# Rows in parity order, so that the first and last DFT steps and the transposes of h run on half-array tiles

## The chip, the cores and the metric

One NeuronCore of a Trainium2 chip. The metric is the device time of one execution in microseconds (us), median over runs. Engines: PE is TensorE, PEld its weight loads, DVE the vector engine, ACT ScalarE, POOL GpSimd; SyncE (SP) issues the DMA transfers. An execution's "span" is the profiled one and is 1 to 2 us shorter than the time. The granted clock is the share of TensorE's full clock that the profile records.

## The reference

2048 rows of 640 numbers in bf16. Two branches share the rows x = q, and a gate mixes them row by row:

```python
k_shift = sum over 4 taps of shifted k * shift_k           # short causal convolution
kv = k_shift * v
y  = irfft(rfft(kv, 2S) * rfft(ssm_k, 2S))[:S] + kv * ssm_D  # long convolution
a  = q * y
h  = gelu(layernorm(x) @ w1); hs = shifted quarters of h @ w2
x1 = x + hs;  b = x1 + gelu(layernorm(x1) @ w3) @ w4
out = g * a + (1 - g) * b,   g = sigmoid(x @ gate_w)
```

The kernel does the transforms as matmuls with tables in four steps: F1 (step 1), T2, I, F4 (step 4). Between steps 1 and 2 and between 3 and 4 the data go out to scratch in DRAM (S_x, S_h, S_g) and are gathered from there in another order. q is loaded a second time for the end; these are the "q reloads".

## The kernel before

Partition p holds the 16 consecutive rows 16p to 16p + 15, so a load takes DRAM in 128 pieces. Step 1 treats even and odd p apart: the table `F1[:, r, :]` has zeros in the rows of the other parity, so each of its matmuls spends all 128 rows and half of them are zeros. Step 4 likewise weaves two results together with a table half of whose columns are zeros. A hand-made list, `ORDER`, fixes the order of all steps.

```python
q_rows = A_q.rearrange("b (p t1) d -> (b p) t1 d", t1=NT)          # k_rows, v_rows, o_rows alike
SP.dma_start(out=X[:, 4*c:4*c+4, :], in_=q_rows[:, 4*c:4*c+4, :])   # 128 rows outermost
...
# h_transpose, per half of 16 steps
for i in range(8):
    PE.transpose(out=ps[:, i, :], in_=hv[:, 8*hh + i, :], identity=IDB[:])
...
# step 1, tasks u < 4 (the fifth has two matmuls of 256 columns)
PE.matmul(ps, lhsT=F1[:, u % 2, :], rhs=src[:, o + 512*(u//2):o + 512*(u//2) + 512], ...)
...
# step 4
for r in range(2):
    PE.matmul(ps[:], lhsT=F4[:, r] (two halves woven, one of them zero), rhs=g[:, r, ... 320], start=(r == 0), stop=(r == 1))
...
def store(t1): SP.dma_start(out=o_rows[:, t1, :], in_=X1[:, t1, :])
def load_q(c): SP.dma_start(out=q2[:], in_=q_rows[:, 4*c:4*c+4, :])   # q again, for the end
```

## Time and profile before

| | before |
|---|---|
| time, median (range) | 250.67 us (250.34 to 251.15) |
| span | 249.1 us |
| V chunk wanted by the vector engine | 32.6 us |
| first product of spectra starts | 123.0 us |
| last product ends | 208.5 us |
| first matmul of step 4 | 223.5 us |
| last vector or ScalarE instruction ends | 246.3 us |

The last five rows are instants read in the trace. They cut the span into stages: front, products, third transforms, tail. With the cuts as windows (columns: stretch, length, busy us of PE, PEld, DVE, ACT, POOL, clock, DMA share, GB/s):

```profile
0.00:20.00 20.00, 7.62 (x104) 6.75 (x105) 16.55 (x53) 14.33 (x22) 1.66 (x11) 1.00 0.91 350
20.00:123.00 103.00, 100.92 (x771) 56.69 (x771) 86.28 (x236) 92.68 (x153) 9.61 (x16) 0.98 0.85 247
...
208.50:223.50 15.00, 15.00 (x101) 8.10 (x99) 5.04 (x8) 3.65 (x4) 0.00 (x0) 1.00 0.38 129
```

TensorE is full from 20 to 123 us and from 208.5 to 223.5; before 20 us the loads are what is full (DMA share 0.91, 350 GB/s).

### The profile page before, as it was taken

How to read it: one execution, taken by the hardware profiler on the slowest of the kernel's cores; microseconds unless marked ns; L12 is line 12 of the kernel's file. 1: busy time of each engine (PE TensorE's matmuls, PEld its weight loads, DVE VectorE, ACT ScalarE, POOL GpSimd, SP SyncE). 2: the span in 40 equal slices, each digit the busy share in tenths (PEclk: the TensorE clock that was granted, in tenths of full speed). 3: DMA queues.
4: the chain of work that ended last, by engine and by line, in shares of the span. 5: the costliest groups of instructions: out<-in, count | busy, mean ns of one | idle time of the engine just before them, and what ended most of it. 6: DMA issues, size and time to landing. Idle time of an engine off the chain costs nothing. (4 is left out here: it accounts for less than half of the span.)

```text
span 249.1 us, 4377 instructions
## 1 busy us (share of the span) xinstructions
PE 227.3 (91%) x1637; PEld 128.6 (52%) x1637; DVE 212.2 (85%) x425; ACT 177.9 (71%) x292; POOL 11.3 (5%) x26
## 2 busy tenths in 40 slices
PE   0746999999999999999999899999989989999994
PEld 0735564444477555444555355555544546546652
DVE  6989998549995999985899999999999997508995
ACT  5599996984699999999988958845678460144530
POOL 1003301000000100031000000000000000000000
PEclk9997999999999999999999999999999999999999
DMA  6999897968858959995997618998403953268773
GB/s 250 377 416 291 189 216 167 240 256 263 241 217 243 387 204 233 346 381 146 183 304 215 204 64 251 186 366 302 132 3 101 342 218 105 105 237 281 222 265 108
DMA packets 50980, 57.65 MB, mean 231 GB/s; under 512 B 25610, under 2 KB 42763, under 8 KB 50703
## 3 DMA queue, kind: packets, MB, share of 16 engines
q1 hardware_dynamic: 50958, 57.38, 74.5%
q8 instruction: 13, 0.21, 0.4%
q14 instruction: 9, 0.07, 0.1%
HBM read 33.77 MB, written 18.36 MB: 209 GB/s over the span
## 5 line engine op out<-in xcount | busy, mean ns | idle before, releaser
L782 PE MATMUL ps<-W,gt 128*128 128x512 bf16 (+1 forms) x384 | 56.6, 299 | 0.0
L764 PE MATMUL ps<-x1t,W 128*128 128x512 bf16 x240 | 55.1, 379 | 0.0
L782 PEld LDWEIGHTS <-gt 128*128 128x128 bf16 x384 | 30.3, 98 | 23.2 <-issue 1.1
L769 ACT ACTIVATE gt<-ps 128x1024 bf16<-128x1024 f32 x24 | 24.5, 1041 | 20.3 <-PE ps L764 20.2
L764 PEld LDWEIGHTS <-W 128*128 128x128 bf16 x240 | 23.3, 98 | 26.4 <-issue 0.3
L323 DVE CAST stg<-ps 128x512 bf16<-128x512 f32 x41 | 26.4, 683 | 5.5 <-PE ps L370 5.3
L639 PE MATMUL psm<-xt,WA 128*128 128x512 bf16 x100 | 23.4, 379 | 0.0
L407 PE MATMUL ps<-ax,TB 128*128 128x512 bf16 (+3 forms) x128 | 22.5, 299 | 0.6 <-DVE hs L323 0.4
L321 ACT CAST stg<-ps 128x512 bf16<-128x512 f32 x39 | 21.7, 602 | 1.2 <-PE ps L370 1.1
L716 PE MATMUL psw<-WA,HT 128*128 128x512 bf16 (+1 forms) x116 | 21.6, 299 | 0.0
L321 ACT CAST gs<-ps 128x512 bf16<-128x512 f32 x29 | 15.2, 599 | 7.5 <-PE ps L446 7.5
L321 ACT CAST xs<-ps 128x512 bf16<-128x512 f32 x27 | 14.7, 617 | 7.0 <-PE ps L407 5.0
L321 ACT CAST hs<-ps 128x512 bf16<-128x512 f32 x27 | 14.2, 601 | 3.2 <-PE ps L407 3.2
L407 PEld LDWEIGHTS <-TB 128*128 128x128 bf16 x128 | 11.6, 98 | 9.2 <-issue 1.9
L784 DVE SCALAR_TENSOR_TENSOR X<-ps,OMG,X 128x640 bf16<-128x640 f32 x16 | 14.0, 877 | 2.4 <-PE ps L782 2.4
L718 DVE SCALAR_TENSOR_TENSOR X<-psw,X 128x640 bf16<-128x640 f32 x16 | 13.1, 819 | 3.3 <-PE psw L716 3.3
L522 PE MATMUL psk<-DG,KT 64*128 64x256 bf16 (+3 forms) x190 | 11.1, 250 | 5.0 <-ACT yk L530 3.7
L815 DVE SCALAR_TENSOR_TENSOR q<-ps,GS,q 128x320 bf16<-128x320 f32 x15 | 7.8, 542 | 9.0 <-PE ps L805 9.0
L639 PEld LDWEIGHTS <-WA 128*128 128x128 bf16 x100 | 9.5, 98 | 11.5 <-issue 0.7
L809 ACT ACTIVATE y<-ps,GS 128x320 bf16<-128x320 f32 x17 | 8.1, 525 | 9.7 <-PE ps L805 7.3
L716 PEld LDWEIGHTS <-HT 128*128 128x128 bf16 x116 | 10.1, 98 | 9.5 <-issue 0.7
L642 ACT ACTIVATE HT<-psm 128x1024 bf16<-128x1024 f32 (+1 forms) x12 | 10.5, 888 | 6.1 <-PE psm L639 5.9
(147 smaller groups left out, 386.3 us busy)
## 6 DMA issues: line engine op xcount, KB each, us to landing
S_x<-stg SPq DMA_DIRECT2D x8, 640.0 KB, 4.3
ax<-S_x SPq DMA_DIRECT2D x8, 640.0 KB, 5.3
S_h<-stg SPq DMA_DIRECT2D x8, 640.0 KB, 9.0
ax<-S_h SPq DMA_DIRECT2D x8, 640.0 KB, 5.3
S_g<-gs SPq DMA_DIRECT2D x8, 640.0 KB, 5.7
W<-in_B_w_dram SPq DMA_DIRECT2D x2, 1920.0 KB
KV<-in_A_v_dram SPq DMA_DIRECT2D x4, 640.0 KB, 11.6
gin<-S_g SPq DMA_DIRECT2D x4, 640.0 KB, 6.5
```

The source lines that it names most:

```text
L321: A.copy(out=dst, in_=src)
L323: V.tensor_copy(out=dst, in_=src)
L407: PE.matmul(ps[:, a - 512 * u:b - 512 * u], lhsT=st["T2"][:, 4 * s + i, :], rhs=ax[:, i, a - i * D:b - i * D], start=True, stop=True)
L522: PE.matmul(ps[e][:, lo:hi, :], lhsT=kt[a], rhs=st["DG"][a, 4 * k + lo - i:4 * k + hi - i, a], start=(i == 0), stop=(i == 7))
L639: PE.matmul(ps[:, v, :].rearrange("p (a b) -> p a b", a=4), lhsT=W1N[:, k, 160 * f:160 * f + P] if f < 4 else W1M[:, k, :], rhs=xt[:, :, k ...
L642: A.activation(out=st["HT"][:, 4 * c:4 * c + 4, 2 * u:2 * u + nf, :].rearrange("p t f b -> p f t b"), in_=ps[:].rearrange("p f (t b) -> p ...
L716: PE.matmul(ps[:, o:o + w], lhsT=h_tile(f, t1), rhs=W2P[:, f, o:o + w], start=(f == 0), stop=(f == 4))
L718: V.scalar_tensor_tensor(out=X1[:, t1, :], in0=ps[:], scalar=1.0, in1=X[:, t1, :], op0=ALU.mult, op1=ALU.add, accum_out=S12[:, 0, t1:t1 + 1])
L764: PE.matmul(ps[:, u, :].rearrange("p (a b) -> p a b", a=4), lhsT=st["W3"][:, k, f * P:(f + 1) * P], rhs=xt[:, :, k, :], start=(k == 0), st ...
L769: A.activation(out=gt[:, 2 * (fp % 2):2 * (fp % 2) + 2, :], in_=ps[:], func=ACT.Gelu_apprx_tanh)
L782: PE.matmul(ps[:, o:o + w], lhsT=st["gt", c, f // 4][:, f % 4, i * P:(i + 1) * P], rhs=st["W4"][:, f, o:o + w], start=(f == 0), stop=(f == ...
L784: V.scalar_tensor_tensor(out=X1[:, t1, :], in0=ps[:], scalar=OMG[:, t1:t1 + 1], in1=X1[:, t1, :], op0=ALU.mult, op1=ALU.add)
```

## The change

The intent is to stop multiplying by zeros. If the even p (blocks of 16 rows) lie in partitions 0 to 63 and the odd ones in 64 to 127, then step 1 is two matmuls of 64 rows on the upper and lower half of the array, side by side, and step 4 two matmuls of 64 columns. For that, every load and store must put the rows in parity order, and the transposes of h must come out so.

```diff
-    q_rows = A_q.rearrange("b (p t1) d -> (b p) t1 d", t1=NT)      # and o_rows, v_rows, k_rows
+    def rows(T, t, n):
+        return bass.AP(tensor=T.tensor, offset=T.offset + t * D, ap=[[NT * D, 2], [2 * NT * D, H], [1, n * D]])
-        SP.dma_start(out=X[:, 4 * c:4 * c + 4, :], in_=q_rows[:, 4 * c:4 * c + 4, :])
+        SP.dma_start(out=X[:, 4 * c:4 * c + 4, :], in_=rows(A_q, 4 * c, 4))     # likewise K, V, q again, out
 h_transpose:
-                    PE.transpose(out=ps[:, i, :], in_=hv[:, 8 * hh + i, :], identity=IDB[:])
+                    for r in range(2):
+                        PE.transpose(out=ps[H * r:H * r + H, i, :], in_=hv[:, 8 * hh + i, r, :], identity=IDB[:], tile_position=(0, H * r))
 step1:
-                    PE.matmul(ps..., lhsT=F1[:, u % 2, :], rhs=src[:, o + 512 * (u // 2):...], ...)
+                for r in range(2):
+                    PE.matmul(ps[r][:], lhsT=F1[H * r:H * r + H, :], rhs=src[H * r:H * r + H, o + 512 * u:o + 512 * u + 512], ...)
 step4:
-                    PE.matmul(ps[:], lhsT=F4[:, r].rearrange("p a b -> p (a b)"), rhs=g[:, r, ...], start=(r == 0), stop=(r == 1))
+                    PE.matmul(ps[H * r:H * r + H, :], lhsT=F4[:], rhs=g[:, r, ...], start=True, stop=True, tile_position=(0, H * r))
# cut: tables F1 and F4 without the zeros, h_shift's copies in parity order, K chunk 0 loaded and transposed
# on TensorE instead of by a transposing DMA, and a new ORDER of all steps
```

H is 64, NT 16, D 640.

## The prediction

The gaps marked in it are passages that no trace or run of this case shows: rules for how many DMA engines a pattern gets and how much tiles gain, and a clause that gave the engines numbers. No term is cut with them: the sum came to 431 us of span, and each of its terms stands in the text. "Two of 16 engines" is the author's estimate, from one load of the kernel before: the W2 tail, with a slowest dimension of 4, had 5 completion events and was in 1.9 us after the load issued before it; by its packets of 55 ns 4 engines would need 1.8 us and 16 engines 0.4.

> **What bounds the kernel now.** I read the page's engine totals and the 40 slices first, then a table by stretches, then the groups by form, the chain, and last the DMA side.
>
> ```profile
> PE 227.3 (91%) x1637; PEld 128.6 (52%) x1637; DVE 212.2 (85%) x425; ACT 177.9 (71%) x292; POOL 11.3 (5%) x26
> PE   0746999999999999999999899999989989999994
> ...
> DMA  6999897968858959995997618998403953268773
> GB/s 250 377 416 291 189 216 167 240 256 263 241 217 243 387 204 233 346 381 146 183 304 215 204 64 251 186 366 302 132 3 101 342 218 105 105 237 281 222 265 108
> ```
>
> TensorE is busy in nine tenths of every slice from 25 us on. Before that the DMA row is full and TensorE is not: the loads set the first 20 us. The stretches say where the vector engine (DVE) is nearly as full:
>
> ```profile
> 10.00:20.00 10.00, 5.53 (x87) 4.65 (x85) 8.78 (x22) 9.97 (x15) 0.45 (x1) 1.00 1.02 412
> ...
> 120.00:200.00 80.00, 77.28 (x491) 41.54 (x489) 77.94 (x78) 57.45 (x97) 0.00 (x0) 1.00 0.72 204
> ...
> 224.00:249.00 25.00, 21.42 (x158) 13.26 (x156) 21.00 (x52) 8.76 (x18) 0.00 (x0) 1.00 0.65 219
> ```
>
> Columns: stretch, length, busy us of PE, PEld, DVE, ACT, POOL, clock, DMA share, GB/s. From 120 to 200 us (the products) DVE has 77.9 of 80 us, as much as PE. In the last 25 us both have 21. The DMA share 1.02 at 412 GB/s says that all 16 DMA engines run without a gap from 10 to 20 us: 412/16 = 25.75 GB/s for each.
>
> ```profile
> DVE 23%; PE 18%; issue 2%; ACT 0%; ACTq 0%; DVEq 0%
> ```
>
> The chain names DVE ahead of PE and covers under half of the span, so I weigh stages, not this list. Its lesson is only that PE time saved will not all come off.
>
> **The work that the change touches on PE:**
>
> ```profile
> L370 PE MATMUL ps<-HT,F 128*128 128x512 bf16 x32 | 10.1, 379 | 0.3 <-ACT stg L321 0.3
> L370 PE MATMUL ps<-KV,F 128*128 128x512 bf16 x32 | 10.0, 379 | 0.6 <-DVE stg L323 0.4
> L805 PE MATMUL ps<-gin,F 128*128 128x320 bf16 x64 | 9.8, 299 | 0.0
> L522 PE MATMUL psk<-DG,KT 64*128 64x256 bf16 x100 | 9.6, 276 | 5.0 <-ACT yk L530 3.7 <-ACT KT L321 1.3
> ```
>
> The means there overlap, so I took start-to-start distances in the trace: 216 ns for 512 columns, 136 for 320, 109 for 256, 63 for a transpose of h. The last row already uses two row tiles (64*128), and there the two partners start 3 ns apart; the column-tiled rows of z start 2 to 4 ns apart. So pairs do run side by side in this kernel.
>
> **The DMA side:**
>
> ```profile
> KV<-in_A_v_dram SPq DMA_DIRECT2D x4, 640.0 KB, 11.6
> ...
> out_dram<-X SPq DMA_DIRECT2D x16, 160.0 KB, 3.1
> ...
> X<-in_A_q_dram SPq DMA_DIRECT2D x3, 640.0 KB, 9.2
> ...
> WA<-in_B_w_dram SPq DMA_DIRECT2D x1, 640.0 KB, 5.6
> ...
> WA<-in_B_w_dram SPq DMA_DIRECT2D x1, 160.0 KB
> ```
>
> Each 640 KB load is 128 packets of 5120 B, 8 on each of 16 engines. A packet of 5120 B takes 196 ns in the trace, of 2560 B 103, of 1280 B 55. The last line shown is the key witness. It loads the tail of W2 through a pattern whose slowest DRAM dimension is 4, not 128:
>
> ```profile
> 44.46 0.58 SPq L171 DMA_DIRECT2D WA<-in_B_w_dram  x1
> 45.08 0.74 SPq L172 DMA_DIRECT2D WA<-in_B_w_dram  x1
> ```
>
> By the trace's landing records the first (640 KB, 128 rows outermost) has 16 completion events and is in at 50.07 us. The second, a quarter as large, has 5 events, the first at once (1.13 us after issue), and is in at 51.96 us, 1.9 us later. On 4 engines its 128 packets of 1280 B are 32 each, 32 x 55 ns = 1.8 us; on 16 they would be 0.4 us.
>
> [...] 16 events for 128 rows, 4 + 1 for the dimension of 4, 1 + 1 for the one-row transfers of z. [...]
>
> **The change part by part.**
>
> 1. Step 1: before 64 matmuls of 512 columns and 32 of 256: 64 x 0.216 + 32 x 0.109 = 17.3 us. After, 40 pairs of row tiles of 512: 40 x 0.216 = 8.6. Saved 8.7 us of PE. Evacuations stay 80 of 512 columns or the like.
> 2. Step 4: 64 x 0.136 = 8.7 us become 32 pairs, 4.35. Saved 4.35, but in the last 25 us, where DVE has 21 us of its own: I count 2.
> 3. Transposes of h: 80 x 63 ns = 5.0 us become 160 of half the size in column pairs: no change if the pairs overlap.
> 4. K's chunk 0 goes through PE: 20 transposes of 56 to 107 ns, +1.1 to 2.1 us, with DVE copies. The new order gives ACT some 8 us more and DVE 4 us less (207 to 208): small.
> 5. Loads and stores. To get the rows in parity order, all loads of X, K, V and q and all stores use a DRAM pattern [2][64][n x 640], on chip 128 partitions. [...] the same bytes on two of 16 engines, 64 packets each. A 640 KB load takes 64 x 196 ns = 12.5 us instead of 1.6; a store 64 x 55 ns = 3.5 us instead of 0.44.
>
> **Front.** Down to the last V load, those two engines get 11 loads of 640 KB (11 x 12.54 = 138.0), two halves of X (2 x 6.7 = 13.4), and their share of W1, the taps' coefficients and the gate (2.2 + 0.36 + 0.36): 154.3 us. With a start at 2.3 us and some latency, the last V chunk is in at about 157.5 us. Before, it was in by 24.7 us. The first DVE instruction that needs it there is one of a tap:
>
> ```profile
> 32.26 0.43 DVE L533 TENSOR_TENSOR KV<-yk,KV 128x512 bf16<-128x512 bf16 x1
> 32.60 0.68 DVE L536 TENSOR_TENSOR KV<-psk,KV 128x512 bf16<-128x512 f32 x1
> ```
>
> 32.6 becomes 157.5: +125 us. Two more taps come after it in the new order than before: +3. What can run meanwhile (statistics, first MLP columns) is little, as its X chunks arrive on the same two engines, the last but for one at 106 and the last at 118 us.
>
> **Middle.** Step 1 gives back 8.7; the saved DVE time of the products about 1. The first q reload [...]: +6 (4 to 8). The third stands ahead of the last gathers for step 4: +8.6.
>
> **Tail.** 16 stores x 3.5 = 56 us plus the last q reload 12.5 = 68.7 us in series on two engines, beginning some 3.5 us into the tail, and about 2 us to land: 74 us against 25.6 now, +49 us. The compute saving of step 4 lies beneath this.
>
> Sum: 249.1 + 125 + 3 - 8.7 - 1 + 6 + 8.6 + 49 = 431 us span, so about 432 us as the time.
>
> **The rivals.**
>
> A. The transfers spread over 16 engines after all. For: bytes and packet sizes are unchanged, and the intent of the change is plain. Then PE loses 8.7 + 4.35 - 1.6 = 11.5 us, of which the DVE-bound products and tail keep a few: 239 to 243 us. Against: the W2 tail's 5 events and 1.9 us.
>
> B. Two engines, but only the front counts: stores and q reloads drain while compute goes on. Then 249 + 125 + 3 - 10 = 367, with some residue 370 to 380. Against: stores begin only when step 4 does, and 56 us of them can't fit into 20.
>
> C. DVE or ACT hides the PE saving and DMA is harmless: 247 to 251 us. For: DVE 77.9 of 80 us in the products. Against: step 1 lies before the products, where PE is the full one.
>
> **Range and chances.** If packets on two lonely engines run a tenth faster, front and tail lose 17 us; if a wait for reused buffers or reordered loads adds, some 20 to 30 more. Between B and that sum I put 385 to 470. A is what speaks for "faster": 0.05. Within 2%: 0.02. Slower: 0.93.
>
> **What would show it.** Three completion events per load and store; DMA share near 2/16 = 0.13 and some 52 GB/s in the first 155 us; PE and DVE idle there, released by the loads of K, X and V; the last V load in at 150 to 160 us; after the last vector instruction still 40 to 50 us of stores. Right in the small: pairs of step 1 and step 4 starting 3 ns apart, 216 and 136 ns between pairs. Wrong if X, K and V land 16-fold by 25 us as before (A or C), or if the last store lands within 5 us of the last vector instruction (B).

## The result, and the profile after

| | before | after |
|---|---|---|
| time, median (range; four executions, one more than above) | 250.91 (250.34 to 252.17) | 453.35 (452.71 to 455.42) |
| span, mean granted clock | 249.1, 0.993 | 452.2, 0.831 |
| V chunk at the vector engine | 32.6 | 159.3 |
| first product | 123.0 | 254.2 |
| last product ends | 208.5 | 349.3 |
| first matmul of step 4 | 223.5 | 377.2 |
| last vector or ScalarE instruction | 246.3 | 428.4 |
| last store in | 248 | 451 |

The ratio of the times is 1.807 (95% interval 1.798 to 1.816). Ratios here are the mean time of one kernel's runs over that of the other's in the same rounds, so not quite the ratio of the medians quoted. Executions over 1.5% slower than the fastest of the same kernel are left out of the means. The page of the changed kernel, totals and slices:

```profile
PE 240.2 (53%) x1721; PEld 128.2 (28%) x1721; DVE 209.8 (46%) x424; ACT 185.0 (41%) x308; POOL 12.4 (3%) x26
...
PE   0020203050032079999999999948999826800600
...
PEclk9999999556557569999999999986999976955655
DMA  1111311111113396549887975952552317111111
GB/s 38 52 53 53 112 52 54 53 53 53 53 52 99 113 185 162 205 176 249 312 277 263 239 220 174 241 179 90 189 177 102 140 49 288 51 50 52 49 49 41
```

Read the two lower rows first: 52 to 54 GB/s in eight of the first ten slices, and 49 to 52 in five of the last six. Before, the first four slices had 250 to 416 and the last six 105 to 281. TensorE is mostly idle in both places, and full, as before, in between. In windows:

```profile
10.00:20.00 10.00, 0.00 (x0) 0.00 (x0) 0.00 (x0) 0.00 (x0) 0.00 (x0) 1.00 0.13 53
100.00:120.00 20.00, 2.28 (x9) 0.70 (x6) 3.56 (x9) 7.85 (x14) 0.00 (x0) 0.59 0.13 53
...
420.00:450.00 30.00, 6.52 (x30) 2.48 (x30) 5.76 (x15) 2.29 (x5) 0.00 (x0) 0.56 0.13 49
```

A DMA share of 0.13 is 2/16, as with two engines full and fourteen idle. 53 GB/s is 2 x 26.5, close to the rate that one engine had before (25.75). The waits of the changed kernel (engine, line, what for; then total us, times, longest) name the same transfers:

```profile
PE pst L536 <- DMA kn<-in_A_k_dram: 91.9, 4, 29.3
...
DVE KV L522 <- DMA KV<-in_A_v_dram: 44.5, 2, 22.7
...
DVE b L600 <- DMA X<-in_A_q_dram: 34.8, 2, 26.8
...
DVE q L801 <- DMA q<-in_A_q_dram: 25.3, 1, 25.3
```

The end of the front is one instruction, in the vector engine's timeline:

```profile
159.31 0.69 DVE L522 TENSOR_TENSOR KV<-psk,KV 128x512 bf16<-128x512 f32 x1 [22.69 <-DMA KV<-in_A_v_dram]
```

And SyncE itself was held, one load after another, for about the time that two engines need for one, 64 packets of 196 ns or 12.5 us (columns: start, us, engine, line, transfer):

```profile
90.72 12.21 SPq L479 DMA_DIRECT2D kn<-in_A_k_dram  x1
102.97 12.21 SPq L490 DMA_DIRECT2D KV<-in_A_v_dram  x1
115.22 12.18 SPq L163 DMA_DIRECT2D GW<-in_gate_w_dram  x1
```

Before, such an issue took 0.3 to 1.5 us. In the landing records (the trace's list of when each completion event of a transfer came) every load of X, K and V, q reload and store with the new pattern has three completion events (one about 1 us after issue or as soon as SyncE is through, two at the end; for the third q reload, issued at 354.90 us, they came at 355.88, 371.21 and 371.31), and the packets of 5120 B still take 196 ns each.

### The profile page after: what moved, and what is told of

Same layout as the page of the kernel before. It is cut to its first block, busy times and chain, and to the rows that moved or that the text cites. A ratio compares the mean times of both kernels' runs of the same rounds, so it can differ in the third digit from the quotient of the medians.

```text
span 452.2 us, 4557 instructions
## 1 busy us (share of the span) xinstructions
PE 240.2 (53%) x1721; PEld 128.2 (28%) x1721; DVE 209.8 (46%) x424; ACT 185.0 (41%) x308; POOL 12.4 (3%) x26
## 4 chain that ended last, share of the span: by engine, by line
PE 32%; SPq 29%; DMA 24%; DVE 8%; ACT 1%; issue 1%; DVEq 0%; ACTq 0%
SPq L154 7%; DMA KV<-in_A_v_dram 7%; PE ps L752 7%; SPq L479 7%; SPq L490 6%; PE ps L770 6%; DMA S_g<-gs 6%; DMA ax<-S_h 5%; PE psw L704 5%; DMA q<-in_A_q_dram 5%; PE psm L625 4%; SPq L157 3%; SPq L163 3%; PE ps L363 2%; PE ps L394 2%; PE pst L336 2%
## 5 line engine op out<-in xcount | busy, mean ns | idle before, releaser
L770 PE MATMUL ps<-W,gt 128*128 128x512 bf16 (+1 forms) x384 | 62.9, 318 | 0.0
L536 PE MATMUL pst<-IDB,kn 128*128 128x128 bf16 x80 | 9.3, 312 | 91.9 <-DMA kn<-in_A_k_dram 91.9
L625 PE MATMUL psm<-xt,WA 128*128 128x512 bf16 x100 | 26.3, 412 | 21.7 <-DVE WA L166 21.7
L536 PEld LDWEIGHTS <-kn 128*128 128x128 bf16 x80 | 8.2, 146 | 92.9 <-DMA kn<-in_A_k_dram 92.9
L312 ACT COPY KT<-pst 128x1024 bf16<-128x1024 bf16 (+1 forms) x9 | 7.4, 873 | 57.7 <-PE pst L536 57.7
L798 ACT ACTIVATE y<-ps,GS 128x320 bf16<-128x320 f32 x21 | 9.8, 525 | 50.9 <-DVE q L801 25.3
L757 ACT ACTIVATE gt<-ps 128x1024 bf16<-128x1024 f32 x24 | 24.6, 1032 | 13.1 <-PE ps L752 12.9
L522 DVE TENSOR_TENSOR KV<-psk,KV 128x512 bf16<-128x512 f32 x12 | 7.9, 678 | 46.2 <-DMA KV<-in_A_v_dram 44.5
L394 PE MATMUL ps<-ax,TB 128*128 128x256 bf16 (+3 forms) x128 | 22.7, 303 | 8.9 <-DMA ax<-S_h 7.8
L793 PE MATMUL ps<-gin,F 128*64 128x320 bf16 x64 | 7.1, 341 | 37.8 <-ACT y L798 25.3
L600 DVE BATCH_NORM_STATS2 b<-X 128x6 f32<-128x320 bf16 x22 | 9.5, 475 | 34.8 <-DMA X<-in_A_q_dram 34.8
L516 ACT CAST yk<-psk 128x512 bf16<-128x512 f32 x8 | 4.5, 582 | 41.8 <-PE psk L508 41.8
```

Source lines behind the costliest of these rows:

```text
L312: A.copy(out=dst, in_=src)
L394: PE.matmul(ps[:, a - 512 * u:b - 512 * u], lhsT=st["T2"][:, 4 * s + i, :], rhs=ax[:, i, a - i * D:b - i * D], start=True, stop=True)
L536: PE.transpose(out=ps[:, i - a, :], in_=src()[:, i * P:i * P + P], identity=IDB[:])
L625: PE.matmul(ps[:, v, :].rearrange("p (a b) -> p a b", a=4), lhsT=W1N[:, k, 160 * f:160 * f + P] if f < 4 else W1M[:, k, :], rhs=xt[:, :, k ...
L757: A.activation(out=gt[:, 2 * (fp % 2):2 * (fp % 2) + 2, :], in_=ps[:], func=ACT.Gelu_apprx_tanh)
L770: PE.matmul(ps[:, o:o + w], lhsT=st["gt", c, f // 4][:, f % 4, i * P:(i + 1) * P], rhs=st["W4"][:, f, o:o + w], start=(f == 0), stop=(f == ...
```

## The experiments

Twelve runs. Those with one look (1, 2, 3 and 11) have one time and an unknown state. The differences of 1 to 3 (36% and more) are far above what states make; that of run 11 (4.9%) is not, and is read by stages below. The gaps marked in the expectations of 5, 6 and 12 are clauses that no trace shows.

### 1. The DMA pattern alone, in the kernel before

```diff
-  in_=q_rows[:, 4 * c:4 * c + 4, :]
+  in_=rows(A_q, 4 * c, 4)        # the change's pattern; likewise halves of X, K chunks 1 to 3, V, q again, out
```

> The kernel before with nothing changed but the DRAM patterns of its loads of X, K and V, its q reloads and its stores: the [2][64] pattern of the change (so the result is wrong on purpose; its order, its tables and its matmuls are those of before). Theory T (two DMA engines): about 430 us, between 410 and 455; three completion events on each of these transfers; last V load in at 140 to 150 us (10 loads of 640 KB, two halves, W1: 141 us), last store some 45 us after the last vector instruction. Rival (the new order or the row and column tiles cost the time): 250 to 255 us.

442.7 us, beside 251.7 for the kernel before. Its first product starts at 241.9 us and the last V load is in at 146.1. Its page shows the same picture with not one tile changed:

```profile
PE 244.4 (55%) x1621; PEld 136.4 (31%) x1637; DVE 213.4 (48%) x425; ACT 179.3 (41%) x292; POOL 11.1 (3%) x26
...
DMA  1111111111491897868899947943372352111111
```

So the pattern alone brings 192 of the 203 us. It loads one 640 KB chunk less on two engines (K chunk 0 still comes by a transposing DMA), and its front is 12.3 us shorter than the changed kernel's: one load of 12.5 us. In the other stages the two differ as well: its tail takes 84.2 us (75.0 in the changed kernel), the products and the stage after them 8 us less. Missed: I expected 45 us of stores after the last vector instruction; there are 28, because the last q reload, in the same queue, delays the vector work itself (22.9 us of waiting for q in its trace). The comparison with the reference passed although the rows were in the wrong order: its tolerance doesn't see the convolution and the shifts here.

### 2, 3 and 4. The pattern split into two transfers of 64 rows, in the changed kernel

```diff
+    def half(T, t, n, r):
+        return bass.AP(tensor=T.tensor, offset=T.offset + (r * NT + t) * D, ap=[[2 * NT * D, H], [1, n * D]])
+    for r in range(2):                                   # for each load (2), each q reload and store (3), or both (4)
+        SP.dma_start(out=dst[H * r:H * r + H], in_=half(T, t, n, r))
```

> The changed kernel, each first load of X, K and V issued as two transfers of 64 rows, 64 outermost, so 16 engines each; q reloads and stores still on two. Theory T: the front gives back 159.3 - 33 = about 126 us, the tail stays: 452 - 126 = 326 us (315 to 340). Rival (the loads were only waiting behind something else): above 400.

> The changed kernel with only the q reloads and the stores of out issued as two transfers of 64 rows each. Theory T: the tail falls from 75 to about 25 us, and the middle gives back 15 to 20 (gathers and S_g stores no longer queue behind q reloads): 452 - 50 - 17 = 385 us (375 to 398). Rival B of the prediction (stores drain under compute): over 430.

> The changed kernel with both. If the two costs add, 452 - 126 - 67 = 259 us. From parts: V at 33, then 92.8 us of TensorE work to the first product (measured in the changed kernel, against 88.8 before), 86 of products, 14.8 to the last step, 22 to 25 of tail: 249 to 252 us. So theory T with the switches of tile mode (some 0.19 us per visit) and transposes that did not pair expects 248 to 258, no faster than before; rival A of the prediction (tiles give 11 us on TensorE) expects 239 to 243.

Measured: 341.3, 387.0 and 273.1 us (269.1 to 274.0; before 251.7). Of the four executions of run 4 two took 269.1 and 272.4, and the profile is of the latter. Stages, from the traces:

| us | front (to first product) | products | to step 4 | tail |
|---|---|---|---|---|
| before | 123.0 | 85.5 | 15.0 | 25.6 |
| after | 254.2 | 95.1 | 27.9 | 75.0 |
| 2, loads halved | 141.3 | 94.8 | 27.8 | 75.6 |
| 3, q reloads and stores halved | 254.0 | 85.5 | 13.2 | 32.5 |
| 4, both | 140.2 | 84.8 | 13.1 | 32.5 |

The parts add. The loads cost the front and hardly anything else; the q reloads and stores cost the products 9.6 us, the stage after them 14.7 and the tail 42.5. Run 3 met its expectation, run 2 missed by a little and run 4 by much: the front is 17 us later than before, not 3. The window from 10 to 20 us of run 4, to be held against the same window of before in the prediction:

```profile
10.00:20.00 10.00, 4.74 (x45) 4.24 (x43) 8.25 (x21) 7.03 (x9) 0.06 (x1) 1.00 1.05 258
```

All 16 engines are full in both (DMA share 1.05 and 1.02), but here they move 258 GB/s, not 412. A tenth of the 5120 B packets takes 388 ns or more; before, a tenth took 202 or more.

### 5 and 6. The second halves from another engine's queue

```diff
-            SP.dma_start(out=dst[H * r:H * r + H], in_=half(T, t, n, r))
+            (A if r else SP).dma_start(...)       # run 5;  (G if r else SP) in run 6; stores alike
```

> The halved transfers of the run before, the second half of each issued from ScalarE's queue instead of SyncE's. In the run with both halves on one queue a packet of 5120 B took up to 387 ns instead of 196: at any time all 16 engines wrote one half of the partitions. Theory P (half of the partitions give half of the rate, both halves at once give the full rate): packets back near 196 to 220 ns, last V load in by about 30 us instead of 42, first product at 33 + 93 = 126 us instead of 140, tail 27 instead of 32: 270 - 14 - 5 = 251 to 256 us[...]. Rival (the doubled packet time comes from small transfers or from DRAM rows that lie apart): still 268 to 274 us and still 387 ns.

> The same with the second halves issued from GpSimd, which is busy only 5% of the time. Theory P: 251 to 258 us. [...] Rival as before: 268 to 274.

276.8 us (276.5 to 277.1) and 269.2 us (267.5 to 271.7), beside 250.7. Theory P missed both; run 6 came out where the rival stood. The window from 20 to 30 us of runs 4, 5 and 6:

```profile
20.00:30.00 10.00, 5.51 (x69) 4.44 (x68) 4.18 (x11) 6.92 (x12) 1.16 (x2) 0.82 1.03 227
20.00:30.00 10.00, 3.08 (x25) 2.54 (x25) 0.39 (x5) 5.08 (x7) 1.22 (x2) 1.00 1.04 227
20.00:30.00 10.00, 2.00 (x38) 1.29 (x34) 1.75 (x5) 4.71 (x10) 0.56 (x2) 0.82 1.05 235
```

The mean 5120 B packet that started there took 366, 370 and 351 ns. Were both halves in flight at once? Counted from the packets between 8 and 40 us, both queues (SyncE's carries other transfers too) had one in flight in half of the time in run 5 and in two thirds in run 6. In these moments the rate was 248 and 251 GB/s, and 227 and 194 in the others. So two queues at once do not bring back the 412 of before. Why not stays open.

### 11. Halves in the kernel before, natural order

(Told here, as it belongs to the same question. "In one piece" in the expectation is not exact: a half still reads 64 pieces of 5120 B, as far apart as in the kernel before, 20 KB, and not 40 KB as in parity order.)

```diff
-        SP.dma_start(out=X[:, 4 * c:4 * c + 4, :], in_=q_rows[:, 4 * c:4 * c + 4, :])
+        for r in range(2):      # X, K chunks 1 to 3, V
+            SP.dma_start(out=X[H * r:H * r + H, 4 * c:4 * c + 4, :], in_=q_rows[H * r:H * r + H, 4 * c:4 * c + 4, :])
```

> The kernel before, with its loads of X, K and V issued as two transfers of 64 rows each, natural order, so DRAM is read in one piece (right result). Theory P (64 partitions at a time give half the rate): packets of 5120 B up to 387 ns, some 230 GB/s from 10 to 30 us, loads in 10 to 17 us later, 258 to 268 us in all. Rival (the rows that lie apart in DRAM are what is slow): 196 ns, 410 GB/s, 250 to 254 us.

262.5 us, and in the same window:

```profile
10.00:20.00 10.00, 8.28 (x83) 7.18 (x83) 5.74 (x10) 7.98 (x10) 0.00 (x0) 1.00 1.05 217
```

This is one execution of unknown state, but its whole loss lies in the front (134.5 us to the first product instead of 123.0), and the later stages take 85.5, 15.0 and 25.6 us as before. The 5120 B packets that started in this window took 379 ns on average, 198 in the kernel before. DRAM is read at the spacing of before and the rate is no better, so parity order's wider spacing is not what is slow. Nor is a transfer of 320 KB as such: in run 9 half a chunk of X, 320 KB on 128 partitions, goes through between 8.6 and 10.1 us, with the DMA engines full, in packets of 102 ns, the same as elsewhere in the trace. What is left, of what was tried, is 64 partitions in one transfer: 217 GB/s with all 16 engines full (share 1.05), where the kernel before has 412. That is reached by elimination; why 64 partitions should be slower no run shows.

### 7. Only the transposes of h in pairs, in the kernel before

```diff
-                    PE.transpose(out=ps[:, i, :], in_=hv[:, 8 * hh + i, :], identity=IDB[:])
+                    for r in range(2):
+                        PE.transpose(out=ps[64 * r:64 * r + 64, i, :], in_=hv[:, 8 * hh + i, 64 * r:64 * r + 64], identity=IDB[:], tile_position=(0, 64 * r))
```

> The kernel before, only the 80 transposes of h as 160 of half the size on two column tiles (the same result, natural order). Theory W (a pair needs two weight loads, which run one after the other, so it takes 111 ns and not 63): 80 x 0.048 = 3.9 us on TensorE, which is full in that stage: 254 to 256 us. Rival, as predicted (pairs overlap, no change): within 1 us of before.

256.6 us (255.3 to 257.0), ratio 1.023 (1.020 to 1.027): slower by itself. The two of a pair start 0 to 6 ns apart, but a pair starts only every 121 ns (every 111 in the changed kernel); a full transpose started every 62. The weight loads of before, and then of this run (busy us, mean ns):

```profile
L344 PEld LDWEIGHTS <-E 128*128 128x128 bf16 x48 | 3.4, 148 | 0.0
```

```profile
L345 PEld LDWEIGHTS <-E 128*64 128x64 bf16 x96 | 6.1, 216 | 0.4 <-issue 0.2
```

Twice as many loads, of half the columns, and each takes longer. These loads read the data that are transposed (E), one load for each full transpose before and one for each half here. Theory W foretold 3.9 us more on TensorE, and the distances from each transpose to the next start sum to 5.2 us more, but its reason, loads one after the other, is not seen: the trace has the two loads of a pair start together (0 to 6 ns apart), and the next two mostly 112 to 123 ns later. Why a pair takes longer than a full transpose stays open. A single transpose that picks the rows by parity does not build: tried in the changed kernel, it stops with "must be a [K, M] pattern with exactly one free dimension", and its operand has two, [16, 2] and [32, 64].

### 8. Only step 4 on column tiles, in the kernel before

```diff
-  PE.matmul(ps[:], lhsT=F4[:, r] (woven), rhs=g[:, r, ...], start=(r == 0), stop=(r == 1))
+  PE.matmul(ps[64 * r:64 * r + 64, :], lhsT=F4C[:, r], rhs=g[:, r, ...], start=True, stop=True, tile_position=(0, 64 * r))
+  # F4C: the two halves of F4 without zeros, two small copies when the table is made
```

> The kernel before, only the last step on two column tiles (its rows then come out in parity order, so the result is wrong on purpose). 32 pairs save 4.35 us of TensorE, some 8 visits of 0.19 us for the change of tile mode take 1.5 back; the vector engine has 21 of that stage's 25 us. Theory: the time falls by 0 to 2 us (249 to 251). Rival (TensorE bounds the tail): it falls by 3 to 4.

252.3 us (251.5 to 252.7), ratio 1.007 (1.004 to 1.010): no gain, a small loss, and a miss for both theories. The tail took 25.1 instead of 25.6 us. The rest of the loss arose before the first product (125.1 instead of 123.0 us), where only the two copies were added; how they cost 2 us was not looked into, and single traces vary as much (the spans of the kernel before run from 247.4 to 250.6).

### 9. The whole change with rows in natural order

```diff
-        return bass.AP(tensor=T.tensor, offset=T.offset + t * D, ap=[[NT * D, 2], [2 * NT * D, H], [1, n * D]])
+        return bass.AP(tensor=T.tensor, offset=T.offset + t * D, ap=[[NT * D, P], [1, n * D]])
```

> The changed kernel with all its order, its tiles and its transposes, but every load of X, K, V, q and every store with the 128 rows outermost as before (so the result is wrong on purpose: the rows no longer lie by parity). It shows what the change is worth when the transfers cost nothing extra. Theory S (the tiles save little: switches of tile mode and half-size transposes give most of it back): V in by 24 to 28 us, first product at 27 + 93 = 120 to 125, products 85, 13 to the last step, 25 of tail: 248 to 254 us. Rival A of the prediction: 239 to 243 us.

250.2 us (249.0 to 251.2), ratio 0.998 (0.995 to 1.002). This is the counterpart of run 1: all of the change but the pattern, and not a microsecond gained. Its page and two of its stages:

```profile
PE 226.7 (91%) x1705; PEld 123.6 (50%) x1721; DVE 208.7 (84%) x424; ACT 184.1 (74%) x308; POOL 12.6 (5%) x26
```

```profile
20.00:124.50 104.50, 101.46 (x848) 53.89 (x853) 84.48 (x241) 95.67 (x162) 9.91 (x14) 0.98 0.80 243
...
223.00:249.00 26.00, 19.60 (x158) 10.20 (x160) 20.21 (x52) 10.67 (x22) 0.00 (x0) 1.00 0.63 205
```

TensorE's total is 226.7 us against 227.3. In the front, where it is full, it has as much to do as before (101.5 and 100.9). In the tail it has 2.3 us less, and the tail is not shorter: the vector engine has 20.2 us of it, 21.0 before.

### 10. The same, with step 1 on full rows

```diff
-   PE.matmul(ps[r][:], lhsT=F1[H * r:H * r + H, :], rhs=src[H * r:H * r + H, o + 512 * u:o + 512 * u + 512], ...)
+   PE.matmul(ps[r][:], lhsT=F1[:], rhs=src[:, o + 512 * u:o + 512 * u + 512], ...)
```

> The run before, with each of the 80 step-1 matmuls on all 128 rows instead of on one of two row tiles (wrong on purpose). Pairs: 40 x 0.222 us, and some 21 visits x 0.187 us for entering and leaving the row-tile mode: 12.8 us. Full rows: 80 x 0.216 = 17.3 us. Theory S: 4 to 5 us slower than the run before. Rival (the pairs save all of the predicted 8.7): 8 to 9 us slower. If the stage is not bound by TensorE: the same.

254.5 us (252.1 to 255.4): 4.3 more than run 9, as expected. So the row tiles of step 1 save about half of the predicted 8.7. Distances between the starts of matmuls of 512 columns, from the trace of run 9 and of before:

| from, to | before | run 9 |
|---|---|---|
| partner of a pair | (no pairs) | 3 ns |
| pair to pair | 216 | 222 |
| MLP matmul, then step 1 | 216 | 311 |
| step 1, then MLP matmul | 216 | 308 |

A visit to the row-tile mode costs 95 + 92 = 187 ns, as much as nine tenths of a matmul of 512 columns, and the order weaves step 1 between MLP matmuls: 21 visits for 40 pairs, 3.9 us. What TensorE does in these 187 ns the trace does not show.

### 12. The same as 9, with the transposes of h at full width

```diff
-                    for r in range(2):
-                        PE.transpose(out=ps[H * r:H * r + H, i, :], in_=hv[:, 8 * hh + i, r, :], identity=IDB[:], tile_position=(0, H * r))
+                    PE.transpose(out=ps[:, i, :], in_=hv[:, 8 * hh + i, :], identity=IDB[:])
```

> The changed kernel with natural rows (the run that equalled before), and the transposes of h back to 80 of full width (wrong on purpose, as there). Theory W [...]: 80 x 0.111 us of pairs + some 0.7 of entering and leaving become 80 x 0.063: 4.5 to 5 us less: 244 to 246.5 us, 1.5 to 2.5% under before. Rival (the stage has another bound by now): 249 to 251.

247.4 us (246.7 to 249.1), ratio to before 0.988 (0.983 to 0.992). A miss by about 1 us: 2.8 less than run 9, not 4.5. The distances from each transpose to the next start add up to 6.5 us here and to 9.6 in run 9, so 3.1 came off; three of the full ones are followed by 0.5 to 0.7 us. It gives a wrong result, as its rows are in natural order, and is no candidate: it only says what the tiles of steps 1 and 4 would be worth if parity order were free. No version with the right result beat the kernel before.

## Why the prediction was right

The time, 453, lies inside the range, 21 above the forecast, and the cause is the one named. By its own steps:

- **Two engines.** Right. Three completion events, a DMA share of 0.13 and 52 GB/s were foretold; the trace has the events, the share and 53 GB/s, and run 1 shows that the pattern alone does it. The estimate from the W2 tail (4 + 1 events at a slowest dimension of 4) carried over to a dimension of 2 (2 + 1 events).
- **Front to the last V chunk: +125.** Measured 159.3 - 32.6 = 126.7. The sum of 11 loads, two halves and the small tables was right to 2 us.
- **From there to the first product: +3 - 8.7.** This failed. It was 90.4 before and 94.9 after: +4.5 instead of -5.7, though the loads of X, K and V are in by then. Its terms: step 1 saves about 4.3 (run 10), not 8.7, as the changes of tile mode were not in the sum; the transposes of h do not cost nothing but about 4.4 us on TensorE (160 with distances summing to 9.4, against 5.0), which run 7 shows alone as 5 to 6 us of time (run 12 gets 2.8 of it back in the new order). TensorE's granted clock is also only 0.86 from 160 to 180 us, after the long idling, where its first MLP columns ran 1.7 us longer than the same 80 matmuls before.
- **Products: -1 + 6.** Measured 95.1 - 85.5 = +9.6. Mechanism right, size short: run 3 takes it off altogether by splitting only q reloads and stores, which the prediction blamed.
- **Last gathers: +8.6.** Measured 27.9 - 15.0 = +12.9. The third q reload and, behind it on the two engines, the last S_g store together took until 372.9 us, and only then were the gathers issued: of that store's 16 completion events 14 were in by 360.1 us, and the last two came at 372.8 and 372.9, after the reload's at 371.2 and 371.3.
- **Tail: +49.** Measured 75.0 - 25.6 = +49.4. The sum of 16 stores and one reload in series was right. "40 to 50 us of stores after the last vector instruction" was wrong: it is 23 (451 - 428), as the last reload held up the vector engine for 25.3 us in the midst of the tail.

Sum: 126.7 + 4.5 + 9.6 + 12.9 + 49.4 = 203.1, which is 452.2 - 249.1. Every term came out larger than foretold (by 1.7, 10.2, 4.6, 4.3 and 0.4), so no two errors hid each other.

Two slips of the prediction change nothing: TensorE is not busy in nine tenths of every slice from 25 us on (three have 8 tenths, the last 4), and 56 + 12.5 is 68.5, not 68.7.

Of the rivals, A (239 to 243 us if the transfers were harmless) fell twice: they are not, and run 9 shows that even then the change stands at 250. C had that number, for another reason: it named the vector engine as what hides the saving, but over the whole program TensorE saved only 0.6 us (run 9); at most the 2.3 us of the tail are hidden by the vector engine, and that is read from busy times, not shown. B fell with the tail.

## What to carry to other kernels

Before a layout is changed through the DRAM side of a transfer, look at its slowest dimension: a 2 there put the loads of X, K, V and q and the stores on two of sixteen engines (DMA share 0.13, 53 GB/s) and cost 192 us (run 1), where the tiles of step 1 gave 4.3 (run 10). Cutting the transfer at that dimension, here at partition 64, gave the engines back (share 1.05 in run 4) but not the rate (258 GB/s instead of 412). And count for a half-array tile the visits to the mode too (187 ns each in run 9), not only the columns, and time a pair before relying on it: 40 pairs in 21 visits kept half of their gain, and transposes in pairs lost (121 ns a pair against 62, run 7).
